# Eight weight chunks moved to another address in SBUF, and another hand-written order for the first fourteen steps, in a fused attention and feed-forward kernel

## The chip, the core and the metric

The kernel runs on one core of one Trainium2 chip. Its time is the device time of one launch in microseconds. Three runs of the kernel before gave 648.92, 650.73 and 651.68 us, median 650.73 us; less is better. Engines are called as in the profile: PE is TensorE's matmul side, PEld its weight loads, DVE VectorE, ACT ScalarE, POOL GpSimd, SP the engine that issues nearly all DMAs.

## What is computed

The reference takes `q`, `k`, `v` of shape (4 batches, 8 heads, 768 positions, 64) in float32 and computes attention with two kinds of keys: the keys less than 16 positions away, and 24 summaries per head, one for each block of 32 positions (the maximum of the block's keys, the mean of its values). The result, 3072 tokens of 512 numbers, goes through a feed-forward layer with a rational function in its middle:

```python
k_sum = k.reshape(B, H, nb, block, D).max(axis=3)
v_sum = v.reshape(B, H, nb, block, D).mean(axis=3)
scores_l = scale * np.matmul(q, k.transpose(0, 1, 3, 2))          # kept where |i - j| < 16
scores_s = scale * np.einsum('bhsd,bhnd->bhsn', q, k_sum) + np.log(block)
a = softmax(concatenate([masked scores_l, scores_s]))
x = a @ concatenate([v, v_sum])                                   # as (3072, 512)
h = x @ w_in                                                      # (512, 2048)
P = a[0] + a[1] * h + a[2] * h2 + a[3] * h3
Q = 1.0 + np.abs(b[0]) * np.abs(h) + np.abs(b[1]) * h2
out = (P / (Q + 1e-06)) @ w_out                                   # (2048, 512)
```

## The kernel before, in words

**Groups and steps.** Tokens are worked in 6 groups of 512, the 2048 inner columns in 16 chunks of 128. One group with one chunk is a step, so there are 96 steps; step n is group n // 16, chunk n % 16. A step multiplies x by the chunk of `w_in` on PE (tile `h`, 12 matmuls of 128x512), applies the rational function (tiles `sq`/`tq`, `ta`, `tu`, `gh`, `gl`; ACT, DVE and POOL share it), and multiplies its result by the chunk of `w_out` (tiles `po`, 4 output tiles of 3 matmuls each, 12 in all). Every operand of these matmuls is in two parts: `xh` and `xl`, `gh` and `gl`, and each weight chunk has a first and a second part, so that three products make up one accurate one. `h` runs 3 steps ahead of `po` (`LAG`).

**Which operand is which.** `pe.matmul(out, lhsT, rhs)` loads `lhsT` as stationary weights and streams `rhs`. In `h` the weight chunk is stationary and `xh` or `xl` streams; in `po` a slice of `gh` or `gl` is stationary and the weight chunk streams.

**Where the chunks lie.** The weights come as float64 words. Functions `w_load` and `w_split` load a chunk (tile `wr`), turn it into float32 in place (ACT, POOL, DVE) and split it into its two parts. Chunks 0 to 7 (`NSTG`) go to one resident tile `wearly`; chunks 8 to 15 go to tiles of the pools `wm` and `wl`, all called `w` in the profile. All six groups use the same 16 chunks. Pools are laid out in the order in which they are opened, and a tile's address follows from the sizes of those before it. In the built program of before, `wearly` begins at byte 14,176 of each partition, which is 352 past a multiple of 512. The other operands of the steps (`w`, `xh`, `xl`, `gh`, `gl`) all begin 224 past a multiple of 512. A chunk takes 8,192 bytes, and every slice that a matmul takes of it begins a multiple of 512 further on.

**Attention.** The 3072 positions are worked in 48 halves of 64 positions (all heads). Halves 0 to 7 make the x of group 0, halves 8 to 15 that of group 1, and so on; so the next group's attention runs between the steps of the present one. A half has scores `sc` on PE, mask and minimum on DVE (`ss`, `sm`), exponential and sum on ACT, a reciprocal on DVE, the normalising on POOL (four TENSOR_SCALAR `ss<-ss,sm`, one for each pair of heads), a transposition on PE (`pt`), a copy to SBUF (`pts`, by DVE or ACT), the product with the values on PE (`av`), and a split of the result into `xh` (ACT or DVE) and `xl` (DVE). From half 16 on the transposition goes over DVE and DRAM instead. One letter of the string `SMODE` for each half says whether ACT takes the minimum away with its exponential (x) or POOL does it ahead (y); `ENG_P` says which engine copies `pts`.

**What sets the order.** `TEXT` is a list of tokens that gives one program order for all engines up to step 13. `h8` is the next piece of half 8, `x2`/`y2` the next piece of step 2's `h`/`po` matmuls, `w3` the next piece of the split of chunk 3, `ga2` to `gk2` the pieces of step 2's rational function, and `K`, `Q`, `W`, `V`, `A`, `I` are loads. A wrapper around each engine (line 105) ties its instructions in that order, so nearly all instructions have line 105 in the profile and are told apart by their tiles. After the list a scheduler orders the rest of steps 14 to 95; only PE keeps the program's order there.

Of the kernel before, what the change touches and what calls it, by code (L numbers as in the profile page):

```python
# [9 lines left out]
F32R = mybir.dt.float32r  # L10
# [37 lines left out]
TEXT = ("K0 K2 k0 Q0 K1 k1 k2 K3 k3 Q1 S0 F0 W0 V0 V1 V2 V5 A9 V3 V6 W1 V4 V7 W2 W3 h0 A8 G0 h0 h0 h1 h1 h0 h3 h1 h2 h4 h0 h4 h6 h1 h5 h2 h0 h1 h1 h4 h3 h2 h0 h6 v0 h3 h2 h2 h0 h2 "  # L48
# [20 lines left out]
SMODE = "xxxyxxxxxxxxxxxx"  # L69
ENG_P = "dddddaadaaadaaaa"  # L70
ENG_X = "daadaaaaaaadaaaa"
MODE = "ccccceceeccccccc"
SQ_PS = "001001001001110"
NHALF = NT // HQ
# [3 lines left out]
def tile_kernel(ctx, tc, qw_in, kraw, kwin, vpad, vred, wio, a, b, cmask, cident, cavg, out):  # L78
    nc = tc.nc
    const = ctx.enter_context(tc.tile_pool(name="const", bufs=1))  # L80
    stage = ctx.enter_context(tc.tile_pool(name="stage", bufs=2))
    sp = ctx.enter_context(tc.tile_pool(name="sp", bufs=4))
# [44 lines left out]
    wearly = const.tile([P, NSTG, 2, 2, DM], F32R, name="wearly")  # L127
# [30 lines left out]
    def key_sum(bi, pr):  # L158
        kr = sums.pop(("k", bi, pr))
        order["k", bi] = order.get(("k", bi), 0) + 1  # L160
        ins = dve.tensor_reduce(ksum[bi][:, pr, :], kr.rearrange("p (n k) -> p n k", k=BLK), axis=AX.X, op=ALU.max)
        if bi:
            tc.keep_in_program_order(ins)
# [602 lines left out]
```

## Time and profile before

| | us |
|---|---|
| median of three runs | 650.73 |
| the profiled execution, its own time | 649.33 |
| its span, first to last instruction | 647.5 |
| PE busy | 625.6 |
| DVE busy | 563.6 |
| ACT busy | 451.9 |
| POOL busy | 254.6 |

The profiled execution took 1.83 us more than its span, which lies around it. It is 1.40 us below the median of the runs. PE's busy time takes an instruction from its start to its modelled end, and matmuls overlap; how fast they follow each other is read from their starts, in the timeline or in the chain of waits, whose pieces run from one instruction's end to the next one's end.

### The profile page before, as it was taken

The numbers are of one execution on the slowest core, as the hardware profiler recorded it, in microseconds if no ns is written. First come the engines' busy times: TensorE is split into PE (matmuls) and PEld (weight loads), VectorE is DVE, ScalarE is ACT, GpSimd is POOL, SyncE is SP. The second block draws the span as 40 slices with busy tenths as digits, with TensorE's granted clock in tenths as the row PEclk, the third lists the DMA queues.
The fourth block names the chain that finished last, engine by engine and source line by source line (L and its number), as shares of the span: only waits on it lengthen the run. The fifth ranks groups of instructions, "written<-read, shape, count | busy, mean of one in ns | idle before, by whom it ended". The sixth has DMA issues, their size and how long they took to land.

```text
span 647.5 us, 11826 instructions
## 1 busy us (share of the span) xinstructions
PE 625.6 (97%) x4068; PEld 496.5 (77%) x4068; DVE 563.6 (87%) x1155; ACT 451.9 (70%) x1006; POOL 254.6 (39%) x354
## 2 busy tenths in 40 slices
PE   8797989999999999999999999999999999999997
PEld 5465767768778887888888888888888888888886
DVE  5689899999989999798998999888888888898985
ACT  3788999978767766866766866756767755655553
POOL 1848478663243244333433334233333231222221
PEclk9998999999999999999999999999999999999999
DMA  9988666603544434244334343223243110100001
GB/s 322 311 290 287 200 202 197 219 26 119 151 150 135 133 117 131 67 147 134 118 99 133 96 141 123 66 71 121 67 134 119 30 64 1 52 14 1 0 2 65
DMA packets 51991, 78.57 MB, mean 121 GB/s; under 512 B 6116, under 2 KB 33124, under 8 KB 50012
## 3 DMA queue, kind: packets, MB, share of 16 engines
q1 hardware_dynamic: 50796, 75.80, 36.0%
q0 software_dynamic: 560, 1.77, 1.5%
q8 instruction: 32, 0.52, 0.3%
q10 hardware_dynamic: 576, 0.25, 0.1%
q14 instruction: 27, 0.22, 0.1%
HBM read 61.31 MB, written 14.73 MB: 117 GB/s over the span
## 4 chain that ended last, share of the span: by engine, by line
PE 72%; DVE 14%; ACT 5%; POOL 5%; issue 3%; DMA 1%; SPq 0%; DVEq 0%; POOLq 0%; ACTq 0%
PE po L105 32%; PE h L105 32%; DVE tu L105 5%; PE sc L105 3%; DVE tq L105 3%; POOL ss L105 3%; PE av L105 3%; DVE gh L105 2%; ACT ta L105 1%; ACT ss L105 1%; DMA kres<-in_kraw_dram 1%; POOL gl L105 1%; PE vf L105 1%; DVE ss L105 1%; ACT wr L105 1%
## 5 line engine op out<-in xcount | busy, mean ns | idle before, releaser
L105 POOL TENSOR_TENSOR gl<-tu,ta 128x512 fp32r<-128x512 f32 x96 | 127.4, 1327 | 331.9 <-DVE tu L105 190.2
L105 PE MATMUL po<-wearly,gh 128*128 128x512 f32 x384 | 121.7, 398 | 0.0
L105 PE MATMUL po<-w,gh 128*128 128x512 f32 x384 | 120.1, 394 | 0.0
L105 POOL TENSOR_SCALAR ss<-ss,sm 128x120 f32<-128x120 f32 x192 | 93.9, 508 | 41.4 <-DVE sm L105 40.4
L105 PE MATMUL h<-xh,wearly 128*128 128x512 f32 x384 | 100.5, 401 | 0.5 <-ACT xh L105 0.5
L105 ACT ACTIVATE ta<-tq,cs 128x512 f32<-128x512 f32 x96 | 69.7, 726 | 41.5 <-DVE tq L105 39.0
L105 PE MATMUL h<-xh,w 128*128 128x512 f32 x384 | 97.1, 391 | 1.5 <-DVE xl L105 1.5
L105 PEld LDWEIGHTS h<-xh,wearly 128*128 128x128 f32 x384 | 72.4, 190 | 18.0 <-issue 0.7
L105 PEld LDWEIGHTS h<-xh,w 128*128 128x128 f32 x384 | 71.8, 188 | 17.5 <-DVE xl L105 2.0
L105 PEld LDWEIGHTS po<-wearly,gh 128*128 128x128 f32 x384 | 71.1, 188 | 17.8 <-issue 1.7
L105 PEld LDWEIGHTS po<-w,gh 128*128 128x128 f32 x384 | 71.1, 188 | 16.1 <-issue 1.3
L105 ACT ACTIVATE ss<-ss,sm 128x120 f32<-128x120 f32 x188 | 71.7, 385 | 16.1 <-DVE sm L105 15.9
L105 DVE SCALAR_TENSOR_TENSOR gh<-tu,cs,ta 128x512 fp32r<-128x512 f32 x96 | 72.4, 755 | 10.5 <-ACT ta L105 2.1
L105 PE MATMUL po<-wearly,gl 128*128 128x512 f32 x192 | 75.9, 395 | 0.0
L105 PE MATMUL po<-w,gl 128*128 128x512 f32 x192 | 75.1, 391 | 0.0
L105 ACT ACTIVATE tu<-h,cs 128x512 f32<-128x512 f32 x96 | 75.0, 781 | 0.0
L105 DVE SCALAR_TENSOR_TENSOR tu<-tu,cs,tq 128x512 f32<-128x512 f32 x96 | 72.0, 750 | 3.0
L105 DVE SCALAR_TENSOR_TENSOR tu<-tu,cs,h 128x512 f32<-128x512 f32 x96 | 70.8, 737 | 1.7
L105 DVE SCALAR_TENSOR_TENSOR tq<-tq,gh 128x512 f32<-128x512 f32 x96 | 66.6, 693 | 2.7
L105 DVE TENSOR_TENSOR tu<-tu,h 128x512 f32<-128x512 f32 x96 | 65.2, 679 | 2.3 <-ACT tu L105 2.1
L105 ACT ACTIVATE ta<-h,cs 128x512 f32<-128x512 f32 x96 | 65.5, 682 | 2.2 <-POOL gl L105 2.2
L105 ACT ACTIVATE sq<-h 128x512 f32<-128x512 f32 x53 | 30.9, 584 | 49.7 <-PE h L105 49.4
(77 smaller groups left out, 923.7 us busy)
## 6 DMA issues: line engine op xcount, KB each, us to landing
wr<-in_wio_dram SPq DMA_DIRECT2D x15, 1024.0 KB
cross<-tb SPq DMA_DIRECT2D x32, 256.0 KB
vw<-in_vpad_dram SPq DMA_DIRECT2D x42, 192.0 KB
kw<-in_kwin_dram SPq DMA_DIRECT2D x40, 192.0 KB
pts<-cross SPq DMA_DIRECT2D x96, 64.0 KB
out_dram<-o SPq DMA_DIRECT2D x24, 256.0 KB
qw<-in_qw_dram SPq DMA_DIRECT2D x40, 128.0 KB
kr<-in_kraw_dram SPq DMA_DIRECT2D x12, 384.0 KB
```

The lines of the kernel that those rows point to most:

```text
L105: out = getattr(self.engine, name)(*args, **kw)
```

## The change

There are three parts that change what the program does.

The first is the address. `wearly` gets a pool of its own (`we`), and that pool and the pool `sp` are opened ahead of `stage`. In the built program `wearly` now begins at byte 16,096, which is 224 past a multiple of 512, as the other operands of the steps do. The staging buffers `st` (tiles `kr`, `vr`, the halves of `wr15`, `vlast`) move from 352 to 224 past a multiple of 512 as well. The pool `sp` (`ks`, `sm`, `vs`) moves as a whole; `qw`, `kw`, `vw`, `ident` and `mask` stay where they were.

The second is another list `TEXT`, with the same pieces of work in another order.

The third is two letters: half 3 has its minimum taken away by ACT and no longer by POOL, and half 11 has its `pts` copied by ACT and no longer by DVE.

The strings `PRODUCT`, `TREE` and `KDMA` are new, and all their letters are 0: the branches that they lead to are not taken, and no instruction comes of them.

```diff
-TEXT = ("K0 K2 k0 Q0 K1 k1 k2 K3 k3 Q1 S0 F0 W0 V0 V1 V2 V5 A9 V3 V6 W1 V4 V7 W2 W3 h0 A8 G0 h0 h0 h1 h1 h0 h3 h1 h2 h4 h0 h4 h6 h1 h5 h2 h0 h1 h1 h4 h3 h2 h0 h6 v0 h3 h2 h2 h0 h2 "
...
+TEXT = ("K0 K2 k0 K1 Q0 k1 k2 K3 k3 S0 Q1 F0 W0 V0 V1 V2 A9 V3 V5 V6 V7 W1 V4 W2 W3 h0 A8 G0 h0 h0 h1 h1 h0 h3 h1 h2 h0 h4 h6 h1 h2 h4 v0 h5 h0 h1 h1 h3 h4 h2 h0 h3 h6 h2 h2 h0 h2 "
...
-SMODE = "xxxyxxxxxxxxxxxx"
-ENG_P = "dddddaadaaadaaaa"
+SMODE = "xxxxxxxxxxxxxxxx"
+ENG_P = "dddddaadaaaaaaaa"
...
+PRODUCT = "00000000000000"
+TREE = "0000"
+KDMA = "00000000"
...
     const = ctx.enter_context(tc.tile_pool(name="const", bufs=1))
+    sp = ctx.enter_context(tc.tile_pool(name="sp", bufs=4))
+    we = ctx.enter_context(tc.tile_pool(name="we", bufs=1))
     stage = ctx.enter_context(tc.tile_pool(name="stage", bufs=2))
-    sp = ctx.enter_context(tc.tile_pool(name="sp", bufs=4))
...
-    wearly = const.tile([P, NSTG, 2, 2, DM], F32R, name="wearly")
+    wearly = we.tile([P, NSTG, 2, 2, DM], F32R, name="wearly")
```

Three places show what the new list does. In the names, the number right behind `sm`, `ss`, `pt`, `pts` or `av` is the half; in `gh0_1` it is group 0, chunk 1; `wr4` is raw chunk 4; the last number only counts tiles.

DVE, behind the reciprocal of half 8, from which POOL normalises half 8. Before:

```order
L105 RECIPROCAL sm8_656<-sm8_656 128x4
L105 TENSOR_REDUCE ks1_664<-kr1_0_665 128x24
L105 TENSOR_TENSOR wearly_102<-wr3_165,wearly_102 128x1024
L105 SCALAR_TENSOR_TENSOR gh0_1_690<-tu0_1_694,cs_95,ta0_1_692 128x512
L105 SCALAR_TENSOR_TENSOR wr4_474<-wr4_474 128x1024
L105 SCALAR_TENSOR_TENSOR tq0_1_693<-tq0_1_693,gh0_1_690 128x512
L105 SCALAR_TENSOR_TENSOR tu0_1_694<-tu0_1_694,cs_95,tq0_1_693 128x512
L105 TENSOR_TENSOR tu0_2_757<-tu0_2_757,h0_2_734 128x512
L105 SCALAR_TENSOR_TENSOR tq0_2_756<-sq0_2_766,cs_95,ta0_2_755 128x512
```

The same piece of DVE's program in the change:

```order
L109 RECIPROCAL sm8_665<-sm8_665 128x4
L109 TENSOR_REDUCE ks1_670<-kr1_0_671 128x24
L109 TENSOR_TENSOR wearly_105<-wr3_168,wearly_105 128x1024
L109 SCALAR_TENSOR_TENSOR gh0_1_696<-tu0_1_700,cs_98,ta0_1_698 128x512
L109 SCALAR_TENSOR_TENSOR wr4_488<-wr4_488 128x1024
L109 TENSOR_TENSOR tu0_2_761<-tu0_2_761,h0_2_738 128x512
L109 SCALAR_TENSOR_TENSOR tq0_2_760<-sq0_2_768,cs_98,ta0_2_759 128x512
L109 SCALAR_TENSOR_TENSOR tq0_1_699<-tq0_1_699,gh0_1_696 128x512
L109 SCALAR_TENSOR_TENSOR tu0_1_700<-tu0_1_700,cs_98,tq0_1_699 128x512
```

The two instructions of step 2 that read `h` or `sq` now stand ahead of the two of step 1 that read `tq`, `gh` and `tu`.

PE, from the transposition of half 14 to its product with the values. Before:

```order
L105 MATMUL pt14_1514<-ident_92,ss14_1361 120x128 x4
L105 MATMUL h0_12_1498<-xl0_453,w12_1464 128x512 x4
L105 MATMUL h0_12_1498<-xh0_452,w12_1464 128x512 x4
L105 MATMUL av14_1558<-pts14_1540,vw0_100 64x64 x8
L105 MATMUL po0_0_817<-w8_1130,gh0_9_1311 128x512 x2
```

In the change:

```order
L109 MATMUL pt14_1518<-ident_95,ss14_1374 120x128 x4
L109 MATMUL po0_3_824<-w8_1139,gh0_8_1249 128x512 x2
L109 MATMUL po0_3_824<-w8_1139,gl0_8_1250 128x512
L109 MATMUL po0_0_821<-w8_1139,gh0_9_1298 128x512 x2
L109 MATMUL po0_0_821<-w8_1139,gl0_9_1299 128x512
L109 MATMUL h0_12_1500<-xl0_456,w12_1468 128x512 x4
L109 MATMUL h0_12_1500<-xh0_455,w12_1468 128x512 x4
L109 MATMUL h0_13_1563<-xh0_455,w13_1549 128x512 x4
L109 MATMUL av14_1568<-pts14_1560,vw0_103 64x64 x8
```

Between the two stood 8 matmuls of 128x512, and now stand 18.

PE, around the transposition of half 10 and its product with the values. Before:

```order
L105 MATMUL po0_2_819<-wearly_102,gl0_2_754 128x512
L105 MATMUL po0_3_820<-wearly_102,gh0_2_753 128x512 x2
L105 MATMUL po0_3_820<-wearly_102,gl0_2_754 128x512
L105 MATMUL pt10_1021<-ident_92,ss10_879 120x128 x4
L105 MATMUL h0_6_1048<-xh0_452,wearly_102 128x512 x4
L105 MATMUL h0_6_1048<-xl0_453,wearly_102 128x512 x4
L105 MATMUL h0_6_1048<-xh0_452,wearly_102 128x512 x4
L105 MATMUL sc12_1069<-kw0_96,qw0_98 64x120 x8
L105 MATMUL av10_1078<-pts10_1046,vw0_100 64x64 x8
```

In the change:

```order
L109 MATMUL po0_2_823<-wearly_105,gl0_2_758 128x512
L109 MATMUL pt10_1026<-ident_95,ss10_877 120x128 x4
L109 MATMUL po0_3_824<-wearly_105,gh0_2_757 128x512 x2
L109 MATMUL po0_3_824<-wearly_105,gl0_2_758 128x512
L109 MATMUL av10_1051<-pts10_1035,vw0_103 64x64 x8
L109 MATMUL h0_6_1061<-xh0_455,wearly_105 128x512 x4
L109 MATMUL h0_6_1061<-xl0_456,wearly_105 128x512 x4
L109 MATMUL h0_6_1061<-xh0_455,wearly_105 128x512 x4
L109 MATMUL sc12_1084<-kw0_99,qw0_101 64x120 x8
```

The transposition stands 3 matmuls of `po` earlier, and 3 matmuls, no longer 12 and the scores of half 12, lie between it and the product.

More of the change, by code (lines that the diff above doesn't have):

```diff
@@ L160, in key_sum @@
         order["k", bi] = order.get(("k", bi), 0) + 1
+        if bi == 1 and TREE[pr] == "1":
+            kr = kr.rearrange("p (n k) -> p n k", k=BLK)
+            half = BLK // 2
+            while half > 1:
+                gps.tensor_tensor(kr[:, :, 0:half], kr[:, :, 0:half], kr[:, :, half:2 * half], op=ALU.max)
+                half //= 2
+            gps.tensor_tensor(ksum[bi][:, pr, :], kr[:, :, 0], kr[:, :, 1], op=ALU.max)
+            return
         ins = dve.tensor_reduce(ksum[bi][:, pr, :], kr.rearrange("p (n k) -> p n k", k=BLK), axis=AX.X, op=ALU.max)
@@ L219, in key_blocks @@
             assert order["k", bi] == NPAIR
-            dve.tensor_copy(kw[jj % 2][:, NKC - 1], ksum[bi])
+            if jj < 2 * HPG and KDMA[jj - HPG] == "1":
+                syn.dma_start(out=kw[jj % 2][:, NKC - 1], in_=ksum[bi])
+            else:
+                dve.tensor_copy(kw[jj % 2][:, NKC - 1], ksum[bi])
     def both_scores(j0):
@@ L502, in gelu @@
         sq = tq
+        product = n < NSTRICT and PRODUCT[n] == "1"
         def a():
             nonlocal sq
+            if product:
+                act.activation(ta, h, AF.Abs)
+                act.activation(tq, ta, AF.Identity, scale=cs[:, 5:6], bias=cs[:, 4:5])
+                return
             if n < start_of(NHALF - 1) + 4 and (n not in halves if n > NSTRICT else n < len(SQ_PS) and SQ_PS[n] == "1"):
@@ L514, in c @@
         def c():
+            if product:
+                gps.tensor_tensor(tq, tq, ta, op=ALU.mult)
+                return
             dve.scalar_tensor_tensor(out=tq, in0=sq, scalar=cs[:, 5:6], in1=ta, op0=ALU.mult, op1=ALU.add)
```

22 rows, old and new, of the table TEXT are left out of this document.

## The prediction

> **What bounds the kernel now.** I read the page first, then busy times by stretches of the program, then the chain of waits, then PE's timeline.
>
> ```profile
> PE 625.6 (97%) x4068; PEld 496.5 (77%) x4068; DVE 563.6 (87%) x1155; ACT 451.9 (70%) x1006; POOL 254.6 (39%) x354
> ...
> 0.00:38.30 38.30, 30.87 (x440) 20.34 (x440) 23.21 (x99) 22.02 (x79) 21.50 (x46) 1.00 0.99 327
> 38.30:140.00 101.70, 93.17 (x588) 69.69 (x588) 94.55 (x190) 90.57 (x182) 69.72 (x61) 0.98 0.63 202
> 140.00:250.00 110.00, 107.80 (x717) 86.62 (x711) 103.61 (x228) 79.96 (x193) 39.01 (x66) 1.00 0.42 128
> 250.00:540.00 290.00, 290.00 (x1882) 235.43 (x1883) 254.47 (x531) 199.69 (x459) 99.01 (x165) 1.00 0.32 101
> ```
>
> The stretches show, after their length, busy us of PE, PEld, DVE, ACT and POOL, the granted clock, and the share and GB/s of the DMAs. Four regimes follow. Up to 38.3 us the DMA engines are full (0.99) and attention fills x of group 0. From there to 140 us (the rest of the hand-written list) PE, DVE and ACT are all near 90%. To 250 us DVE is at 94%. From 250 us on PE never idles (290.00 of 290.00) and DVE has 12% to spare: there the time is the number of matmuls times their pace, and a slower or faster pace is felt in full.
>
> The chain of waits gives that pace. Its columns are start, length and engine; a piece of x12 is one step's `h` or `po`:
>
> ```profile
> 544.44 2.73 PE po L105 x12
> ...
> 577.78 2.80 PE po L105 x12
> ...
> 591.76 2.73 PE h L105 x12
> 594.50 2.79 PE po L105 x12
> ...
> 608.34 2.73 PE h L105 x12
> 611.08 2.72 PE po L105 x12
> ...
> 632.84 10.89 PE po L105 x48
> ```
>
> Twelve matmuls of the same shape at full clock take 2.80 us in one place and 2.72 in another (233 and 227 ns apiece; the last 48 go at 10.89 / 48 = 227 ns). PE's timeline, which has the tiles' names, says which is which:
>
> ```profile
> 574.82 2.03 PE L105 MATMUL h<-xh,wearly 128*128 128x512 f32 x8
> 577.62 0.63 PE L105 MATMUL po<-wearly,gh 128*128 128x512 f32 x2
> 580.41 1.33 PE L105 MATMUL h<-xh,wearly 128*128 128x512 f32 x5
> ...
> 613.64 1.98 PE L105 MATMUL h<-xh,w 128*128 128x512 f32 x8
> 616.36 0.62 PE L105 MATMUL po<-w,gh 128*128 128x512 f32 x2
> 619.08 1.98 PE L105 MATMUL h<-xh,w 128*128 128x512 f32 x8
> ```
>
> A step whose `h` and `po` both use `wearly` takes 580.41 - 574.82 = 5.59 us, one with `w` in both 619.08 - 613.64 = 5.44. Both tiles have the same shape, type and partners. What differs is where they begin: `wearly` 352 past a multiple of 512, `w` and every partner 224.
>
> **The change part by part. The address.** If the offset is the cause, all matmuls go at the pace of `w`. From 544.44 to 611.08 lie 24 pieces, among them all 16 that use `wearly` in the last group: 66.64 us, where 24 x 2.72 are 65.28. So a group is worth 1.36 us. Groups 2 to 5 lie behind 250 us, where PE is the bound: 4 x 1.36 = 5.44 us, taken whole; with PE faster by that, DVE's 254.47 us would stand in 284.6, still with room. In group 1 (140 to 250 us) PE twice waits for DVE:
>
> ```profile
> 169.77 0.45 PE L105 MATMUL av<-pts,vw 120*64 120x64 f32 x8 [0.60 <-DVE tu L105]
> 249.93 2.14 PE L105 MATMUL h<-xh,w 128*128 128x512 f32 x8 [1.53 <-DVE xl L105]
> ```
>
> What PE gains ahead of the second wait it may lose in it, since DVE is late there and not PE. Bounds 0 and 1.36; I take half, 0.7. In group 0 the same bounds hold, and DVE (94.55 of 101.7) and ACT (90.57) leave less; I take 0.3. Address together: 6.4 us, from 5.4 to 8.2 if the offset is the cause.
>
> The same move puts DVE's split of a chunk on equal offsets. It costs nothing, as these two show, one with unequal offsets and one with equal, neither beside POOL:
>
> ```profile
> 39.59 1.23 DVE L105 TENSOR_TENSOR wearly<-wr,wearly 128x1024 fp32r<-128x1024 f32 x1 [0.53 <-ACT wearly L105]
> ...
> 140.04 1.22 DVE L105 TENSOR_TENSOR w<-wr,w 128x1024 fp32r<-128x1024 f32 x1
> ```
>
> The Trainium skill speaks against this part. In "TensorE: Matmul & The Clock Gate", section "Step-by-step: what each phase is for", it says that PE has two independent SBUF read ports and that "Loading the next tile's weights doesn't steal SBUF read bandwidth from the running matmul." By it no address could matter, and this term would be 0. The trace's two paces don't fit that sentence taken plainly, but nothing in the trace shows that the offset makes them.
>
> **The list.** I size the places that the rows of before let me size.
>
> First loads. The key block of pair 1 now goes ahead of half of `qres` (512 KB). DVE waits for a key block here:
>
> ```profile
> 8.72 2.67 DVE L105 TENSOR_REDUCE ks<-kres 128x24 f32<-128x768 f32 x3 [3.19 <-DMA kres<-in_kraw_dram]
> ```
>
> At the 327 GB/s of this stretch 512 KB are 1.6 us, so two of the three maxima (0.89 each) can be done before the last block lands. At best the three end one maximum sooner; `qres` lands later, but the scores also need the last maximum. Bounds 0 and 0.9; I take 0.4.
>
> Half 8. PE's longest idle time behind the start:
>
> ```profile
> 14.30 1.39 POOL L105 TENSOR_SCALAR ss<-ss,sm 128x120 f32<-128x120 f32 x4 [13.85 <-DVE sm L105]
> ...
> 53.06 5.34 POOL L105 TENSOR_SCALAR ss<-ss,sm 128x120 f32<-128x120 f32 x4
> ...
> 57.24 0.32 PE L105 MATMUL pt<-ident,ss 128*120 128x128 f32 x1 [3.44 <-POOL ss L105]
> 58.58 2.06 PE L105 MATMUL h<-xh,wearly 128*128 128x512 f32 x4
> 62.80 0.63 PE L105 MATMUL po<-wearly,gh 128*128 128x512 f32 x2
> ...
> 56.35 0.68 DVE L105 SCALAR_TENSOR_TENSOR tq<-tq,gh 128x512 f32<-128x512 f32 x1
> 57.74 0.68 DVE L105 TENSOR_TENSOR tu<-tu,h 128x512 f32<-128x512 f32 x1
> ```
>
> POOL's four take 1.39 us alone and 5.34 here, beside a run of DVE instructions with two inputs from SBUF. The second of the four lets PE go on at 57.24, just behind the end of DVE's `tq<-tq,gh` (56.35 + 0.68 = 57.03), and the last ends (58.40) while DVE has one input from SBUF and one from PSUM (`tu,h`). The new list puts those (57.74 and the next) ahead of the pair that begins at 56.35. So POOL can go on at 56.35 instead of 57.03: 0.7 us, at most the pair's 1.39 (57.74 - 56.35), at least 0. The pair is late by as much, then `gl` of step 1, which by PE's order is needed only behind 36 more matmuls: hidden. Behind the wait the 12 matmuls of `h` take 62.80 - 58.58 = 4.22 us where 2.80 are normal, because the granted clock falls:
>
> ```profile
> 56.00:60.00 4.00, 2.21 (x6) 1.58 (x7) 3.96 (x8) 3.89 (x13) 3.91 (x5) 0.77 0.98 316
> ```
>
> If the shorter wait also kept the clock, another 1.4 us would go; I don't take it, and keep it as the far bound. The skill (same page, "HAM oscillation — how this bites in real kernels") lets the clock drop after idle gaps over about 3.4 us. By that the 1.4 would go too, since 3.44 - 0.7 lies under it. The trace agrees as far as the 3.44 us gap stands ahead of the 0.77; it has no shorter gap so close to tell.
>
> Half 14. PE waits for the `pts` copy:
>
> ```profile
> 131.71 0.69 PE L105 MATMUL av<-pts,vw 120*64 120x64 f32 x16 [0.80 <-ACT pts L105]
> ```
>
> With 18 matmuls in between instead of 8, 10 x 0.23 = 2.3 us more cover it: 0.8 us, bounds 0 and 0.8.
>
> Half 10. Against these, its transposition comes 3 matmuls (0.7 us) earlier on PE, and there PE already waited for POOL:
>
> ```profile
> 83.31 0.33 PE L105 MATMUL pt<-ident,ss 128*120 128x128 f32 x1 [0.99 <-POOL ss L105]
> ...
> L105 ACT COPY pts<-pt 120x512 f32<-120x512 f32 x9 | 5.3, 592 | 0.0
> ```
>
> That wait grows by up to 0.7, and the copy of `pts` (592 ns on ACT) has only these 0.7 of cover. Behind it on PE stand step 6's `h` and all of step 3's `po`. I take +0.7; bounds 0 and 1.4.
>
> The two letters. Half 3 loses the first three rows, and ACT takes it pair by pair as it does the other halves; half 11's copy (677 ns) goes from DVE to ACT:
>
> ```profile
> L105 POOL TENSOR_TENSOR ss<-ss,sm 128x480 f32<-128x480 f32 x1 | 1.0, 990 | 0.0
> L105 ACT ACTIVATE ss<-ss 128x480 f32<-128x480 f32 x1 | 0.6, 604 | 0.9 <-POOL ss L105 0.9
> L105 DVE TENSOR_REDUCE sm<-ss 128x4 f32<-128x480 f32 x1 | 0.6, 641 | 0.0
> ...
> L105 DVE COPY pts<-pt 120x512 f32<-120x512 f32 x7 | 4.7, 677 | 1.7 <-PE pt L105 1.7
> ```
>
> Up to 38.3 us ACT is busy 22.02 of 38.30 us, which hides half 3's part; without that cover it could be 1.0 either way. 0, bounds -1 and +1. Half a dozen more pairs on DVE, ACT and PE trade places without a row that sizes them: 0, bounds -2 and +2. The list comes to -0.4 - 0.7 - 0.8 + 0.7 = -1.2.
>
> **Sum**, against the profiled execution: 649.33 - 6.4 - 1.2 = 641.7. That execution is 1.40 below the median of the runs, so I forecast 643.1 us.
>
> **The rivals.**
>
> *A: the offset isn't the cause.* `wearly` also lies at the low end of each partition (14,176 to 79,712) and all partners above 114,400, and stays there. Then only the list acts: 650.73 - 1.2 = 649.5.
>
> ```profile
> L105 PE MATMUL av<-pts,vw 120*64 120x64 f32 x672 | 25.3, 226 | 2.4 <-ACT pts L105 1.8 <-DVE tu L105 0.6
> L105 PE MATMUL av<-pts,vr 120*64 120x64 f32 x64 | 2.7, 228 | 1.0 <-issue 0.5 <-DVE xl L105 0.5
> ```
>
> For it: no matmul in the trace has an operand low at offset 224, and the small `av` matmuls are alike with values at 352 (`vw`) and at 224 (`vr`) past a multiple of 512. Against it: all eight chunks of `wearly`, 64 KB apart at the ends, go at one pace, and `w` over 64 KB at another. The skill's sentence above stands on this side. Chance 0.17.
>
> *B: DVE is the bound up to 250 us and eats all there.* Then the list and groups 0 and 1 give nothing: 650.73 - 5.4 = 645.3. For it 103.61 of 110 and the wait at 249.93; against it the waits on POOL and ACT that the list relieves. Chance 0.18.
>
> *C: everything counts.* 8.2 of address, the list with the clock kept: 650.73 - 8.2 - 2.6 = 639.9. Chance 0.09.
>
> *D, slower: the new list makes PE wait for POOL in the halves 10 to 15.* They stand where PE, DVE and ACT are full. If each `pt` came to PE ahead of POOL's four, by as much as half 8 did (3.44 us, and 1.4 of clock), six halves would cost 29 us; slower by over 0.5% than before takes 6.4 + 3.3 = 9.7 us, so two in full or all six by 1.6 us. For it: half 10's earlier place. Against it: halves 14 and 15 get more work ahead. At six times 1.8: 650.73 - 6.4 + 10.8 = 655. Chance 0.09.
>
> **How the numbers follow.** My case has 0.47, its own range 641 to 645.3. Over 0.5% (3.25 us, about what a measurement of this kernel tells from no change) faster means under 647.5: nearly all of my case, B and C, and a little of A. Faster 0.73, same 0.18, slower 0.09. The range from 639.2 to 650.5 takes in C, B and A; D is left out.
>
> **What would show it.** In the chain of waits of the last group every piece at 2.72, and the steps 5.44 us long with `wearly` as with `w`; if 2.80 stays, A holds. From 250 us to the end the new trace should take 5.4 us less than the 397.5 of before. The wait at half 8 should be near 2.7 us, that at half 14 gone, that at half 10 near 1.7, and the wait for `xl` ahead of group 2 up to 1 us longer. I am wrong if the gain behind 250 us is missing, or if it is there and the list gives back more than 3 us.

## The result: 646.3 us, and where the profile after differs

Five runs of the changed kernel have a median of 646.3 us (644.32 to 648.14), five of the kernel before on the same chip 650.7 us (648.92 to 651.68). The ratio is 0.9937, with a 95% interval from 0.991 to 0.9965: 4.4 us faster (the interval reaches from 2.3 to 5.9) where 7.6 were forecast. The profiled execution took 646.6 us, its span is 644.8.

First the page of the changed kernel, busy time by engine and the chain of waits by engine, then the same four stretches as before (length; busy us of PE, PEld, DVE, ACT, POOL; granted clock; DMA share and GB/s):

```profile
PE 622.1 (96%) x4068; PEld 496.1 (77%) x4068; DVE 567.9 (88%) x1152; ACT 452.4 (70%) x1015; POOL 251.6 (39%) x353
...
PE 49%; DVE 30%; ACT 7%; POOL 6%; issue 5%; DMA 2%; DVEq 0%; SPq 0%; POOLq 0%
```

```profile
0.00:38.30 38.30, 31.86 (x445) 21.07 (x446) 23.59 (x99) 23.95 (x88) 21.49 (x45) 1.00 0.98 320
38.30:140.00 101.70, 93.67 (x580) 69.68 (x580) 95.56 (x187) 90.64 (x183) 65.42 (x61) 0.97 0.62 205
140.00:250.00 110.00, 107.18 (x721) 85.85 (x715) 103.88 (x224) 77.91 (x192) 38.51 (x64) 1.00 0.40 126
250.00:540.00 290.00, 288.40 (x1888) 236.40 (x1889) 258.34 (x536) 201.61 (x463) 101.34 (x169) 1.00 0.32 102
```

Two things are to be seen. Behind 250 us PE is no longer busy all the time (288.40 of 290.00 where it was 290.00). Most of these 1.60 us, 1.15, are no new loss: the wait for `xl` that ended at 249.93 us before ends at 251.15 now, on the other side of the border. The rest is idle time that was not there before. And the granted clock from 38 to 140 us is 0.97, not 0.98, though the wait at half 8 was to shrink.

The chain of waits of the last group in the changed kernel shows the address part at work:

```profile
553.84 2.72 PE po L109 x12
...
578.32 2.72 PE h L109 x12
...
594.64 2.72 PE h L109 x12
...
630.00 10.99 PE po L109 x48
```

Every piece from 553.84 to 630.00 is 2.72 us long, with `wearly` as with `w`; the 2.80 pieces of before are gone.

PE's timeline of the changed kernel has the waits that answer to those of before (the bracket tells the idle time ahead of an instruction and what ended it):

```profile
53.84 0.32 PE L109 MATMUL pt<-ident,ss 128*120 128x128 f32 x1 [1.06 <-POOL ss L109]
55.67 0.81 PE L109 MATMUL pt<-ident,ss 128*120 128x128 f32 x2 [1.50 <-POOL ss L109]
56.13 2.06 PE L109 MATMUL h<-xh,wearly 128*128 128x512 f32 x4
...
61.40 0.67 PE L109 MATMUL po<-wearly,gh 128*128 128x512 f32 x2
...
82.03 0.32 PE L109 MATMUL pt<-ident,ss 128*120 128x128 f32 x1 [1.50 <-POOL ss L109]
...
125.32 1.16 PE L109 MATMUL h<-xh,w 128*128 128x512 f32 x4 [0.92 <-DVE tu L109]
...
251.15 1.19 PE L109 MATMUL h<-xh,w 128*128 128x512 f32 x4 [1.53 <-DVE xl L109]
...
391.11 2.14 PE L109 MATMUL h<-xh,wearly 128*128 128x512 f32 x8 [0.33 <-DVE xl L109]
```

Half 8 now waits 1.06 and 1.50 us instead of 3.44 and 0.54, half 10 1.50 instead of 0.99 and 0.45, and half 14's 0.80 has gone, but 0.92 of waiting for `tu` stands at 125.32. The last row is new: a wait for DVE in the stretch where PE had none. This is the operation that PE waits for there, in DVE's timeline:

```profile
390.38 0.68 DVE L109 TENSOR_TENSOR xl<-av,xh 128x512 fp32r<-128x512 f32 x1
```

To follow the difference along the program, the table takes the start of the first `po` matmul of a step from PE's timeline, as the profiled execution less that of before. Step 24 is the middle of group 1, step 56 that of group 3. The table has the experiments too, whose edits follow. The ratios are each against the kernel before on the same chip; the experiments ran on four chips, so the medians of two rows are best compared by their ratios. The starts and the span are those of the one profiled execution, whose own time stands beside the median, and which isn't always a typical one: that of the list alone was the quickest of 12, that of the changed kernel with half 8 filled the second of six, that with halves 8 to 11 filled the slowest of six.

| kernel | median us | profiled us | ratio to before (95%) | step 0 | step 3 | step 24 | step 56 | span |
|---|---|---|---|---|---|---|---|---|
| before | 649.54 to 650.7 | 649.33 | 1 | 62.80 | 88.72 | 226.49 | 423.72 | 647.51 |
| changed | 646.3 | 646.6 | 0.9937 (0.991 to 0.9965) | -1.41 | -1.17 | +0.86 | -0.22 | -2.72 |
| address alone | 646.2 | 646.62 | 0.9952 (0.9933 to 0.9971) | +1.09 | +1.25 | +1.14 | -0.10 | -2.68 |
| list alone | 649.87 | 647.13 | 1.0007 (0.9994 to 1.002) | -4.25 | -4.48 | -2.50 | -2.19 | -2.17 |
| address, half the list | 646.51 | 646.17 | 0.9959 (0.9944 to 0.9974) | -2.90 | -2.99 | +0.30 | -0.51 | -3.12 |
| before, VectorE light | 647.17 | 647.24 | 0.9957 (0.994 to 0.9974) | +0.16 | -0.57 | -1.36 | -2.10 | -2.08 |
| address, VectorE light | 642.02 | 641.7 | 0.9881 (0.9857 to 0.9905) | +0.56 | -0.31 | -1.84 | -5.12 | -7.60 |
| before, half 8 filled | 648.8 | 648.82 | 0.9984 (0.9969 to 1.0) | -0.32 | -0.35 | -0.43 | -0.52 | -0.48 |
| address, half 8 filled | 646.11 | 645.15 | 0.993 (0.9906 to 0.9955) | -2.71 | -1.12 | -0.37 | -1.58 | -4.15 |
| changed, half 8 filled | 644.71 | 642.27 | 0.992 (0.9895 to 0.9945) | -4.26 | -4.46 | -3.43 | -4.56 | -7.03 |
| changed, halves 8 to 11 filled | 643.72 | 645.19 | 0.9902 (0.9884 to 0.992) | -2.69 | -2.52 | -0.50 | -1.60 | -4.11 |
| changed, half 8 filled, GpSimd | 644.6 | 644.68 | 0.9921 (0.99 to 0.9941) | -3.95 | -4.10 | -0.55 | -2.00 | -4.62 |

The row of the changed kernel reads: 1.2 us ahead at step 3, 0.9 behind at step 24, and from there 3.58 us gained to the end (from +0.86 to -2.72). So what the first 225 us were to bring is missing, and a part of what the rest was to bring.

### The profile page after: what moved, and what is told of

It reads as the page before. It is cut to its first block, busy times and chain, and to the rows that moved or that the text cites. A ratio compares the mean times of both kernels' runs of the same rounds, so it can differ in the third digit from the quotient of the medians.

```text
span 644.8 us, 11844 instructions
## 1 busy us (share of the span) xinstructions
PE 622.1 (96%) x4068; PEld 496.1 (77%) x4068; DVE 567.9 (88%) x1152; ACT 452.4 (70%) x1015; POOL 251.6 (39%) x353
## 4 chain that ended last, share of the span: by engine, by line
PE 49%; DVE 30%; ACT 7%; POOL 6%; issue 5%; DMA 2%; DVEq 0%; SPq 0%; POOLq 0%
PE po L109 22%; PE h L109 22%; DVE tu L109 10%; DVE tq L109 8%; POOL ss L109 4%; DVE gh L109 4%; PE sc L109 2%; DVE ss L109 2%; PE av L109 2%; ACT ta L109 2%; DMA kres<-in_kraw_dram 1%; ACT ss L109 1%; POOL gl L109 1%; DVE wr L109 1%; DVE ks L109 1%
## 5 line engine op out<-in xcount | busy, mean ns | idle before, releaser
L109 POOL TENSOR_TENSOR gl<-tu,ta 128x512 fp32r<-128x512 f32 x96 | 129.7, 1351 | 328.7 <-DVE tu L109 208.9
L109 POOL TENSOR_SCALAR ss<-ss,sm 128x120 f32<-128x120 f32 x192 | 90.2, 491 | 43.8 <-DVE sm L109 40.7
L109 ACT ACTIVATE ss<-ss,sm 128x120 f32<-128x120 f32 x192 | 73.2, 387 | 15.5 <-DVE sm L109 15.3
L109 ACT ACTIVATE ta<-ta 128x512 f32<-128x512 f32 x96 | 60.8, 633 | 2.9
```

Source lines behind the costliest of these rows:

```text
L109: out = getattr(self.engine, name)(*args, **kw)
```

## The experiments

Two theories stood at the start. T1: DVE sets the pace up to 250 us, and swallows there what PE gains, from the address as from the list; further on some of the gain is lost because DVE is late. T2: the new list itself costs what the first 225 us should have gained.

### The parts apart

The address alone:

```diff
-    stage = ctx.enter_context(tc.tile_pool(name="stage", bufs=2))
     sp = ctx.enter_context(tc.tile_pool(name="sp", bufs=4))
+    we = ctx.enter_context(tc.tile_pool(name="we", bufs=1))
+    stage = ctx.enter_context(tc.tile_pool(name="stage", bufs=2))
...
-    wearly = const.tile([P, NSTG, 2, 2, DM], F32R, name="wearly")
+    wearly = we.tile([P, NSTG, 2, 2, DM], F32R, name="wearly")
```

> The kernel before with the moved pools alone: the eight early chunks begin at 224 past a multiple of 512, as their partners do; order list and letters stay. The forecast's sum has the whole address term and none of the list's: 650.7 - 6.4 = 644.3. Theory T1 (DVE sets the pace up to 250 us and swallows the gain of groups 0 and 1, whatever the list; behind it some of the gain is lost to `xl` coming late): as the change itself, 646 to 647, with start of step 28 within 0.5 us of before's. Theory T2 (the new list loses what groups 0 and 1 gain): start of step 28 about 1 us earlier than before's, 643.5 to 645. In both, the pieces of 12 matmuls in the last group are 2.72 us.

The list and its two letters alone, with the pools of before:

```diff
-TEXT = ("K0 K2 k0 Q0 K1 k1 k2 K3 k3 Q1 S0 F0 W0 V0 V1 V2 V5 A9 V3 V6 W1 V4 V7 W2 W3 h0 A8 G0
...
+TEXT = ("K0 K2 k0 K1 Q0 k1 k2 K3 k3 S0 Q1 F0 W0 V0 V1 V2 A9 V3 V5 V6 V7 W1 V4 W2 W3 h0 A8 G0
...
-SMODE = "xxxyxxxxxxxxxxxx"
-ENG_P = "dddddaadaaadaaaa"
+SMODE = "xxxxxxxxxxxxxxxx"
+ENG_P = "dddddaadaaaaaaaa"
```

> The kernel before with the new order list and its two letters alone; the early chunks stay at 352 past a multiple of 512. The forecast's sum has the list at -1.2: 649.5. T1 (DVE sets the pace up to 250 us): what the list moves is swallowed too, 650.2 to 651.2. T2 (the new list costs in steps 3 to 28): the 1.4 us that it gains up to step 3 are lost and 1 to 2 us more, 651.7 to 653. In all, pieces of the last group at 2.73 to 2.80 us as before.

The address, with the new list up to the token `gi3` (270 tokens, in which both lists hold the same pieces of work) and the old one behind it. Beside the diff of the address alone:

```diff
-TEXT = (the old list)
+TEXT = (tokens 1 to 270 of the new list, tokens 271 to 562 of the old)
-SMODE = "xxxyxxxxxxxxxxxx"
+SMODE = "xxxxxxxxxxxxxxxx"
```

> The address part, and of the new list the first 270 entries alone (up to step 4 and `gi3`), then the old list. T1: no better than the change, 646 to 647. T2: the early 1.4 us stay and the later loss is gone, 642.5 to 644; step 3 starts 1.2 to 1.5 us before the old kernel's, step 28 about 2 us before it. The forecast's sum (address 6.4, first loads 0.4, half 8 0.7; halves 10 and 14 as in the old list) would be 643.2.

The address alone gives 646.2 us, by its ratio 3.1 us (1.9 to 4.4), where the change gave 4.1 (2.3 to 5.9): the two can't be told apart. In its trace step 28 starts 1.43 us behind that of before, where I had expected it within 0.5 us (T1) or 1 us ahead (T2); 1.09 of that was there at step 0 already, behind a longer fall of the clock at half 8, and from step 0 to step 28 it lost 0.34. The list alone gives nothing that can be told from zero: between 0.4 us faster and 1.3 us slower. The third kernel decides between T1 and T2: it has the old list from step 4 on, starts step 3 2.99 us ahead and has lost all of it, and 0.3 more, by step 24. PE's waits from 140 to 250 us in that kernel (us in total, times, longest) show into what the lead turned:

```profile
PE av L105 <- DVE tu L105: 2.2, 3, 0.9
PE h L105 <- DVE xl L105: 1.4, 2, 0.9
PE po L105 <- ACT o L105: 1.3, 1, 1.3
```

That is 4.9 us. Before it was 2.1 in the same stretch, but 1.5 of that is the wait that ends at 249.93 us, which this kernel has behind 250; like for like it is 4.9 against 0.6. So 3.6 us of the waits are for DVE, and 1.3 for a copy of ACT (`o`). The new list's later part is not what eats the lead, since the old one in its place eats as much; T2 falls. The one trace of the list alone lost 1.98 us from step 3 to step 24 and the changed kernel's 2.03. That DVE is what swallows an early lead of the list is read from such waits; the list was not run with a lighter DVE.

### The offset

Eight tiles of one chunk each, with gaps of 32 bytes, so that each chunk begins at another distance from its partners:

```diff
-    wearly = we.tile([P, NSTG, 2, 2, DM], F32R, name="wearly")
+    wearly = []
+    for i in range(NSTG):
+        wearly.append(we.tile([P, 2, 2, DM], F32R, name="w" + "abcdefgh"[i]))
+        we.tile([P, 8], F32, name=f"gap{i}")
...
-        return wearly[:, fc] if fc < NSTG else wlate[fc]
+        return wearly[fc] if fc < NSTG else wlate[fc]
```

> The changed kernel with eight tiles of one chunk each, 32 bytes left free behind each: chunks 0 to 7 begin 256, 288, 320, ... 480 bytes (modulo 512) past where their partners begin. If the offset within 512 bytes is the cause and only equality is quick, all eight chunks run 12 matmuls in 2.77 to 2.80 us in the last group; if the price goes with the distance, it rises from chunk 7 (32 bytes before its partners) to chunk 0 (256); if rival A holds and the offset is not the cause, all show 2.72 as in the changed kernel. For the whole time: 646 where all are quick, 650 to 652 where none is.

The second kernel puts the same eight tiles between `kw0` and `kw1` in the pool `const`:

```diff
-    kw = [const.tile([P, NKC, NPAIR, NB], F32, name=f"kw{i}") for i in range(2)]
+    kw = [const.tile([P, NKC, NPAIR, NB], F32, name="kw0")]
+    wearly = []
+    for i in range(NSTG):
+        wearly.append(const.tile([P, 2, 2, DM], F32R, name="w" + "abcdefgh"[i]))
+        if i < NSTG - 1:
+            const.tile([P, 8], F32, name=f"gap{i}")
+    kw.append(const.tile([P, NKC, NPAIR, NB], F32, name="kw1"))
```

> As the run before it with eight single chunk tiles, but placed so that chunks 0 to 7 begin 32, 64, 96, 128, 160, 192, 224 and 256 bytes (modulo 512) past where their partners begin. In the run before it the chunk 256 bytes away alone was quick (226.6 ns from one matmul of `h` to the next, the seven others 230 to 235). If only the distance modulo 256 counts: chunk 7 at 226.6 to 227, chunks 0 to 6 at 230 to 235. If that chunk was quick for its absolute place (224 past a multiple of 512) instead: chunk 7, now at 192, is slow. If distances of 64 or 128 are quick as well, chunks 1, 3, 5 show it.

The pace is read from starts. Of the first kernel's PE timeline in the last group (`wa` is chunk 0, 256 bytes from its partners, `wb` 288; between the start of a row of 8 and that of the next lie 8 matmuls):

```profile
546.83 1.98 PE L109 MATMUL h<-xh,wa 128*128 128x512 f32 x8
548.64 1.07 PE L109 MATMUL h<-xl,wa 128*128 128x512 f32 x4
...
552.28 2.02 PE L109 MATMUL h<-xh,wb 128*128 128x512 f32 x8
554.14 1.10 PE L109 MATMUL h<-xl,wb 128*128 128x512 f32 x4
```

And of the second (`we` 160, `wh` 256):

```profile
568.71 2.03 PE L108 MATMUL h<-xh,we 128*128 128x512 f32 x8
570.58 1.09 PE L108 MATMUL h<-xl,we 128*128 128x512 f32 x4
...
585.43 1.99 PE L108 MATMUL h<-xh,wh 128*128 128x512 f32 x8
587.26 1.07 PE L108 MATMUL h<-xl,wh 128*128 128x512 f32 x4
```

Eight matmuls take 1.81 us at a distance of 256 (226 ns each), 1.86 at 288; in the second kernel 1.87 at 160 and 1.83 at 256. The other distances of the two kernels, 32, 64, 96, 128, 224, 320, 352, 384, 416 and 480, take 1.86 or 1.87 by the same rows of their chunks; 192 takes 1.84, as 448 does. So the offset is the cause (rival A falls), only the distance modulo 256 counts, and each of the distances tried that is not zero costs about the same 3%, at 192 half of that. These are the matmuls of `h`, where the chunk is stationary. In `po`, where it streams, the same two traces have the half price at 64 and 320 instead (230 ns from start to start, where the other distances have 233 and 192 and 448 too): in both it is where the streaming operand begins 64 past the stationary one, modulo 256. My own expectation was half wrong here: I had looked for a period of 512. The chunk at 256 was at 224 past a multiple of 512 in one kernel and at 192 in the other, so its own place is not what counts. The times of the two, one run each, are 648.96 and 648.66 us, between that of the changed kernel and that of before, with one chunk of eight quick.

### VectorE's load

Both kernels leave out the two operations of `j` (0.69 and 0.75 us on DVE) in steps 0 to 71, so `gl` is made from an unfinished `tu` and the output lacks that correction. They differ only by the address:

```diff
         def j():
+            if n < 72:
+                return
             dve.scalar_tensor_tensor(out=tq, in0=tq, scalar=C1 * SH, in1=gh, op0=ALU.add, op1=ALU.mult)
```

> The kernel before without the two vector operations of `j` (the rounding remainder of the product) in steps 0 to 71, 0.69 + 0.75 us of VectorE in each: `gl` is then made from a stale `tu`, so that part of the computation is left out. It is the partner of the next run. T1 and its rival alike: the VectorE waits of TensorE (1.5 us at 250 us, 0.6 at 170 us) go; 644 to 649.

> The address part alone, with the same vector operations left out in steps 0 to 71. T1 (the address gain not seen in the time was swallowed by waits for VectorE): with VectorE light the whole gain of 6.4 to 7.6 us shows, so this run is 5.5 to 7.5 us below its partner, and the profile shows no TensorE wait for `xl` or `tu` between 150 and 400 us. If VectorE is not the cause: 3 to 4 us below the partner, as the address alone is below the kernel before.

The pair differs by 5.15 us (647.17 and 642.02), where the address alone had brought 3.3 on a full DVE (medians). That is less than the 5.5 to 7.5 that I had expected of T1 and more than the 3 to 4 without it; since the address alone may be worth up to 4.4 us, the two times hardly decide. The traces do. The stretch from 250 to 540 us in the kernel of the pair without the address part:

```profile
250.00:540.00 290.00, 290.00 (x1883) 235.46 (x1882) 234.37 (x446) 200.77 (x462) 95.95 (x159) 1.00 0.31 98
```

And in the one with it:

```profile
250.00:540.00 290.00, 290.00 (x1900) 238.43 (x1899) 237.19 (x450) 202.77 (x465) 96.64 (x159) 1.00 0.31 98
```

All of PE's waits from 140 to 540 us in the one with it (us in total, times, longest):

```profile
PE h L106 <- DVE xl L106: 1.0, 1, 1.0
```

And the same of the address alone with DVE full:

```profile
PE h L106 <- DVE xl L106: 2.1, 3, 1.5
PE av L106 <- DVE tu L106: 1.3, 2, 0.9
```

With DVE at 82% (237.19 of 290.00) instead of 89%, PE is busy all the time behind 250 us at the quicker pace, and waits once for 1.0 us from 140 us on instead of five times for 3.4. In the table the pair's address gain is 0.88 us from step 0 to step 24 (from +0.40 to -0.48) and 5.04 from there to the end; on a full DVE it was 0.05 backwards and 3.82. Both traces of the pair have the clock at half in the same two places, so it doesn't tell them apart. T1 holds for the address: what it loses on a full DVE it keeps on a light one. One reservation: behind the hand-written list a scheduler orders the steps, so leaving work out may also have moved some.

### The clock at half 8

The changed kernel waits less at half 8, and yet its `h` behind it takes 61.40 - 56.13 = 5.27 us, longer than the 4.22 of before. Stretches of 2 us of the changed kernel (the granted clock stands ahead of the last two numbers):

```profile
54.00:56.00 2.00, 0.50 (x2) 0.18 (x1) 2.00 (x4) 1.95 (x5) 1.95 (x2) 0.66 1.01 339
56.00:58.00 2.00, 2.00 (x7) 1.61 (x7) 1.97 (x4) 1.97 (x10) 1.16 (x1) 0.50 1.00 352
58.00:60.00 2.00, 2.00 (x6) 1.62 (x5) 2.00 (x4) 1.98 (x3) 1.29 (x1) 0.50 0.86 330
60.00:62.00 2.00, 2.00 (x7) 1.53 (x7) 2.00 (x4) 0.74 (x2) 1.92 (x1) 0.63 0.10 38
```

In the trace of the list alone PE's timeline has one wait of 2.82 us at the same place:

```profile
54.92 1.00 PE L105 MATMUL pt<-ident,ss 128*120 128x128 f32 x3 [2.82 <-POOL ss L105]
```

The stretch behind it shows no fall:

```profile
56.00:58.00 2.00, 2.00 (x10) 1.64 (x9) 1.96 (x4) 1.97 (x8) 0.74 (x1) 1.00 0.96 356
```

The clock's records in the traces explain the difference in part. Behind 20 us every stretch of one clock lasts a whole multiple of 3.41 us, except the last, which the end cuts off, and the borders between the pieces of 3.41 us lie at another place of the program in each execution. The half clock lasts from 54.64 to 61.47 us in the changed kernel, from 58.13 to 61.55 before. The piece ahead of the fall in the changed kernel, and the two pieces over which the long wait of the list alone is spread:

```profile
51.23:54.64 3.41, 1.59 (x5) 0.38 (x3) 3.41 (x6) 3.38 (x7) 3.31 (x4) 1.00 0.62 193
...
50.11:53.53 3.42, 1.67 (x5) 0.40 (x3) 3.42 (x7) 3.36 (x8) 3.33 (x3) 1.00 0.57 170
53.53:56.94 3.41, 1.99 (x9) 1.40 (x10) 3.41 (x5) 3.33 (x12) 3.13 (x4) 1.00 1.03 348
```

PE is idle for 1.82 us of the first (3.41 - 1.59), and for 1.74 and 1.42 of the others. Over all 14 traces there are nine falls between 20 and 630 us; in the piece ahead of each PE was idle for 1.68 to 3.17 us, and in every other piece at full clock for 1.58 at most, except the 1.74 of the list alone. So in these traces it is the idle time within one such piece that goes with a fall, about half of it, and not the length of a wait; the same waits can fall into one piece in one execution and into two in the next. It isn't the whole rule: three traces have a fall at about 12 us, behind pieces with 1.23 to 1.41 us of idle time.

To see what the fall costs, the waits were filled with matmuls whose results are overwritten; PE still waits for POOL, but isn't idle. On the changed kernel, with 17 of them:

```diff
+        fill = weights(0)[:, 0, 0, :]
         for pr in range(NPAIR):
+            for _ in range((1, 5, 11, 0)[pr] if jj == HPG else 0):
+                pe.matmul(pt[:, pr * P:], fill[:, 0:P], fill[:, pr * P:], start=True, stop=True)
             pe.transpose(out=pt[:NK, pr * P:(pr + 1) * P], in_=att[jj][:, pr, :], identity=ident)
```

> The changed kernel, with 17 matmuls of early weights into the not yet written part of `pt8` ahead of its first three transposes: their results are overwritten, and they fill the three waits of 0.28, 1.06 and 1.50 us at 52 to 57 us. If the waits cause the half clock that follows them (0.50 to 0.66 from 54 to 62 us in the changed kernel's trace, none in the list-alone trace), the granted clock stays at 1.00 there, step 0 starts 2.5 to 3 us earlier, the mean clock is 0.999 or 1 in every run, and the time is that of the changed kernel's one run at 0.999: 644.0 to 644.8. If DVE swallows what is gained ahead of 250 us: clock at 1.00 all the same, 645.5 to 646.5. If the half clock has another cause: clock 0.992 to 0.997 and 646.3.

The same on the kernel before, with other counts for its other waits:

```diff
+            for _ in range((1, 19, 4, 0)[pr] if jj == HPG else 0):
```

> The kernel before, with 24 matmuls of early weights into the not yet written part of `pt8` ahead of its transposes, which fill the waits of 0.21, 3.44 and 0.54 us at 53 to 58 us: TensorE still waits for GpSimd there, but is not idle. If the waits lower the clock behind them: granted clock 1.00 in 54 to 64 us instead of 0.53 to 0.61, step 0 starts 1.5 to 2 us earlier in the trace, median 1.5 to 2.5 us under the kernel before. If the clock falls for another reason: no change, 649.5 to 651.

The same line and counts on the kernel with the address part and the old list:

> The address part with the old order list, and half 8's waits filled as in the kernel before with the fill. It closes a square of four: old list without and with the address part (648.8 and this), old and new list with both (this and 644.7). If the terms add up, the address part is worth the 3.3 us here that it was worth without the fill, 645.5, and the list 0.8 us. If the list's early gain (1.4 us at step 3) survives where the clock is held, the list is worth more: 646 to 647. If the list is worth nothing: 644.2 to 645.

And on the changed kernel with halves 8 to 11 filled:

```diff
+        count = {HPG: (2, 6, 12, 0), HPG + 1: (0, 2, 4, 0), HPG + 2: (0, 0, 0, 13), HPG + 3: (0, 2, 4, 0)}.get(jj, (0,) * NPAIR)
+            for _ in range(count[pr]):
```

> The changed kernel with more of the same matmuls: half 8's waits filled to the end, and those of halves 9 (0.36 and 0.55 us), 10 (0.83) and 11 (0.40 and 0.46). With half 8 filled alone, two of six runs had a mean clock of 0.999 or 1 (641.9 and 642.3) and four had 0.996 or 0.997 (644.7 to 645.5). If the clock still fell in those four because of what stayed idle at halves 8 to 11: all runs at 0.999 or 1, median 642 to 642.8. If it fells elsewhere in the program: a mix of clocks as before, 643.5 to 645.

In PE's timeline of the first (the changed kernel with half 8 filled), the waits are down to 0.19 and 0.20 us, and `h` takes 58.54 - 55.72 = 2.82 us:

```profile
53.45 0.33 PE L109 MATMUL pt<-ident,ss 128*120 128x128 f32 x1 [0.19 <-POOL ss L109]
...
55.28 0.66 PE L109 MATMUL pt<-ident,ss 128*120 128x128 f32 x2 [0.20 <-POOL ss L109]
55.72 1.16 PE L109 MATMUL h<-xh,wearly 128*128 128x512 f32 x4
...
58.54 0.62 PE L109 MATMUL po<-wearly,gh 128*128 128x512 f32 x2
```

The stretch at the same place has the clock at 1.00:

```profile
56.00:58.00 2.00, 2.00 (x10) 1.64 (x9) 1.96 (x3) 1.97 (x9) 0.77 (x1) 1.00 1.00 369
```

Its six runs: 641.9 and 642.27 us at a mean clock of 1.0 and 0.999, and 644.68 to 645.51 at 0.996 or 0.997. So the clock still fell somewhere in four of them, where I had expected it in none. PE's timeline of the address part with half 8 filled shows where that can be, at half 10, whose waits are not filled:

```profile
80.64 0.33 PE L106 MATMUL pt<-ident,ss 128*120 128x128 f32 x1 [1.24 <-POOL ss L106]
81.40 0.32 PE L106 MATMUL pt<-ident,ss 128*120 128x128 f32 x1 [0.44 <-POOL ss L106]
```

The clock there, in stretches of 4 us of the same kernel:

```profile
80.00:84.00 4.00, 2.92 (x9) 2.20 (x10) 3.96 (x8) 3.97 (x13) 3.18 (x4) 0.73 0.56 233
84.00:88.00 4.00, 4.00 (x41) 3.03 (x40) 1.91 (x3) 1.76 (x5) 3.44 (x6) 0.84 0.50 94
```

With halves 8 to 11 filled, all six runs have a mean clock of 0.999 or 1. These are half 8 and halves 10 and 11 of that kernel's trace:

```profile
52.00:62.00 10.00, 8.23 (x51) 6.57 (x51) 9.96 (x13) 8.56 (x19) 8.34 (x7) 1.00 0.69 229
76.00:92.00 16.00, 15.74 (x102) 11.91 (x101) 14.09 (x29) 13.75 (x28) 11.98 (x14) 1.00 0.50 159
```

So waits there make the clock fall, and keeping PE at work prevents it. What it is worth in time is less sure: 643.72 us is 1 us more than I had expected of it (642 to 642.8), and the interval of its ratio, 0.9902 (0.9884 to 0.992), still meets that of the change (0.991 to 0.9965). Its ratio is the lowest of the kernels that compute the whole result, 0.98% under the kernel before, though not to be told from that with half 8 filled alone (0.992). On the kernel before, the fill is worth 0 to 0.31%, 1.0 us by the medians, where I had expected 1.5 to 2.5; its clock was 1.00 behind half 8, as expected, but in the profiled execution 0.91 in the first 38.3 us, so step 0 started only 0.32 us earlier. With half 8 filled and the address part in both, the old list has 0.993 and the new one 0.992, which is no difference. The old list's 646.11 us lies where I had put it if the list were worth more (646 to 647); its runs were on another chip, and its interval (0.9906 to 0.9955) covers most of the new one's (0.9895 to 0.9945).

### Some of VectorE's work to GpSimd

The values stay the same; every second step from 14 to 62 gives the last operation of `j` to POOL, on the changed kernel with half 8 filled:

```diff
+            if 14 <= n < 64 and n % 2 == 0:
+                gps.tensor_scalar(tu, tu, cs[:, 0:1], 1.0, op0=ALU.add, op1=ALU.mult)
+                gps.tensor_tensor(tu, tu, tq, op=ALU.subtract)
+                return
             dve.scalar_tensor_tensor(out=tu, in0=tu, scalar=cs[:, 0:1], in1=tq, op0=ALU.add, op1=ALU.subtract)
```

> The changed kernel with half 8's waits filled, and the last operation of `j` (`tu<-tu,cs,tq`, 0.75 us on VectorE) done by GpSimd in two operations in every second step from 14 to 62: the same values, with VectorE 0.75 us lighter per two steps. If VectorE's load is what holds back the address gain behind 150 us: the waits for `xl` and `tu` there (0.4 to 1.5 us at 166, 241, 247 and 387 us) shrink, 1 to 2 us under the kernel with the fill alone (644.7): 642.5 to 643.7. If GpSimd's longer chain makes `gl` late, or slows VectorE: 645 to 648.

It measured 644.6 us (0.9921), as the fill alone (644.71, 0.992): nothing won, and between the two ranges that I had named. DVE from 250 to 540 us fell to 253.31 us, from the changed kernel's 258.34, but between 150 and 250 us PE waited longer for DVE than with the fill alone (1.44 us at 167 and 1.43 at 173 us, where it had 1.23 and none). The lead at step 3 was 4.10 us, and 0.55 at step 24. So here a DVE that was 5 us less busy behind 250 us did not help as leaving the work out did. That POOL's longer chain is what made the waits longer was not tested.

## Why the prediction was right, and where not

The forecast was 643.1 us, the time is 646.3: inside the range and on the side foretold, 3.2 us off. It lies outside the range of my own case (641 to 645.3) and is inside the whole range only because that took in rivals B and A; rival B's 645.3 came nearest. The mechanism of the address was right, the sizes of the terms were too large. Point by point, by the steps of the prediction:

- **The cause of the two paces** was right, and rival A falls. All pieces of the last group are at 2.72. The Trainium skill's sentence in "TensorE: Matmul & The Clock Gate", section "Step-by-step: what each phase is for", that loading weights doesn't steal read bandwidth from the running matmul, would have set this term to 0; the runs show 226 ns for a matmul at distances of 0 and 256 and about 233 at others, so for these operands the address does count. What in the chip makes it so, no run here shows.
- **Groups 2 to 5, "taken whole", 5.44 us.** This step failed in part. From the last `h` of group 1, the one behind the wait for `xl`, to the end the new trace takes 644.8 - 251.15 = 393.6 us, the old one 397.6: 4.0 less. With DVE light the same stretch brings 5.04 from step 24 on, near the term, which was 0.4 us too large. The reason that I gave for taking it whole, that DVE's 254.47 us would still have room in 284.6, was the mistake. PE doesn't wait for DVE's share of busy time but for single operations in its line: the row at 391.11 waits for `xl<-av,xh`, the operation that frees the PSUM tile that `h` needs. By the starts of `po`, all that is lost behind step 32 is lost in two steps: step 42 takes 6.03 us and step 50 6.24, where both take 5.58 with DVE light. In both, `xl<-av,xh` ends just ahead of the late `h` (390.38 + 0.68 = 391.06 at step 50). The condition that I set for being wrong (gain behind 250 us missing) is not met, but a quarter of it is.
- **Groups 0 and 1, 0.3 and 0.7 us.** Measured alone on a full DVE, from step 0 to step 24: nothing. With DVE light: 0.88. I had named what could eat it and taken half; it ate all, though not where I had looked: the wait for `xl` at 250 us stayed at 1.53, and the new waits for `tu` and `xl` stand ahead of it. This is rival B's mechanism, which the light pair shows for the address.
- **The list, -1.2 us.** Measured alone: -0.4 to +1.3. Its single terms went otherwise than sized, mostly for the better. PE's wait for the scores in the first loads fell from 2.06 to 0.91 us (forecast 0.4 less). Half 8's waits fell by 1.4 us together (3.44 + 0.54 to 1.06 + 1.50; forecast 0.7). Half 10 came out even (1.44 to 1.50; forecast +0.7). Half 14's 0.80 went, as forecast, but 0.92 of waiting for `tu` came at 125.32, so next to nothing was left of it. All of these gains lie ahead of step 24, and by then the trace of the list alone had lost 1.98 us of its 4.48, the changed kernel's all of its lead: the error was to add waits of PE up as time in a stretch that another engine paces, after giving the address a discount for just that. What rival B said of the list holds by its time; that DVE is the reason is read from the waits alone.
- **The clock.** I didn't take the 1.4 us that a shorter wait might have given back. That came out right in the changed kernel's trace, where the fall was longer, not gone; but I had no reason for it, and in the trace of the list alone there is no fall. As far as these traces show, where the borders of the 3.41 us pieces lie in an execution decides with the waits whether one comes, so this was luck as much as judgement. The Trainium skill's threshold (same page, "HAM oscillation — how this bites in real kernels", idle gaps over about 3.4 us) does not agree with these traces: the clock fell amid gaps of 1.06 and 1.50 us and behind gaps of 1.24 and 0.44, and not behind one of 2.82. Its next section, "A second HAM failure mode: psum-queue depth-cycling", speaks of short idle times in a row that make the clock oscillate; that stands nearer to what the traces show.
- **Rival D** did not come: none of halves 10 to 15 waits for POOL longer than half 10's 1.50 us.

What the terms come to: the address is worth 3.1 to 3.3 us on this kernel's DVE (1.9 to 4.4 by the interval), about 5 where DVE is light; the list is worth nothing that these runs can tell. How much of an early lead survives to step 24 varies from trace to trace (from step 3 on 1.0 us was lost with half 8 filled, 2.0 in the changed kernel, 3.3 with half the list, 3.6 with work moved to GpSimd); what decides that was not found. The two letters alone were not tried.

## What to carry to other kernels

Where the same matmul shows two paces in the timeline, compare where its two SBUF operands begin: here a distance that is not a multiple of 256 bytes costs up to 3% of each matmul, and opening a pool at another place mends it. A quicker engine gains its full time only if the engines that free its buffers are ahead at those places, as PE's two late steps show; look for the operation that frees the tile, not at the share of busy time. Before adding up waits that a new order removes, ask which engine paces the stretch in which they lie, and check by making that engine lighter.

## What the runs showed of the hardware that was not expected

- The pace of a 128x512 matmul depends on the distance between the starts of its two SBUF operands, modulo 256 bytes. In `h`: 226 to 228 ns at 0 and 256, 232 to 234 at 32, 64, 96, 128, 160, 224, 288, 320, 352, 384, 416 and 480, and 230 at 192 and 448 (8 matmuls in 1.84 us). In `po`, with the roles of the chunk exchanged, the 230 stand at 64 and 320.
- PE's granted clock went to 0.50 for 6.8 us amid waits of 1.06 and 1.50 us, and stayed at 1.00 behind a single one of 2.82. It changed on borders 3.41 us apart, whose place in the program differs between executions; between 20 and 630 us each fall came behind a piece of 3.41 us with at least 1.68 us of idle time. With those waits filled by matmuls of no use, all six runs of one kernel had a mean clock of 0.999 or 1, while of 17 runs of the kernel before on the same chip none had over 0.997.
- Half the clock for 6.8 us costs about 3 us of PE's time: the list alone, without the fall in its trace, was 2.84 us ahead of the changed kernel at step 0. What of it reaches the end differs. With half 8 filled, the two runs at a mean clock of 0.999 or 1 took 641.9 and 642.27 us and the four at 0.996 or 0.997 644.68 to 645.51; with halves 8 to 11 filled, all runs at 0.999 or 1 took 643.36 to 645.19.
